# List schedule of a gated mix kernel: rank of the gate scores, planned transfer rate and slack behind a landing

## The chip, the core and the metric

The kernel runs on one core of a Trainium2 chip. The metric is the device time of one execution in microseconds (us). TensorE is called PE, VectorE DVE, ScalarE ACT, GpSimd POOL and SyncE SP, as in the profile; SP and POOL are here the queues that start transfers.

## The reference

With x = A_u of 2048 tokens and 512 channels, the reference computes a gate per token, a long convolution per channel (S4D), and a bilinear GLU of width 1792, and mixes the two:

```
g = sigmoid((x * gate_w).sum(-1))
K = 2 * Re(sum_n C * dt * exp(A * dt * pos))        # per channel, 128 states, 2048 positions
a = irfft(rfft(K, 4096) * rfft(x.T, 4096))[:2048].T + x * D_skip
b = ((x @ w_gate) * (x @ w_up)) @ w_down
out = g * a + (1 - g) * b
```

## The kernel before

Two streams of work share the engines. The GLU is the larger. Its products run in three passes of a high and a low part of each operand: per tile of hidden units, `pg` and `pu` are sums over four 128-row pieces kt of `xs,wlo` and `xs,whi` (three matmuls of 128x512 for each piece, 0.227 us from start to start), ACT copies pg into h, DVE multiplies h by pu, ACT casts h to hh, and DVE subtracts (`hl<-h,hh`). Then `y` collects `dhi,hl`, `dlo,hh` and `dhi,hh` for each of the hidden tiles of a group. There are two banks for y, one each for pg and pu, and four for all that is named `k`. ACT evicts y as `acc<-y,ngate`, scaled by 1 - g of its token rows, so the first evictions wait for the gate. Tokens come as `raw` or `ts`, are split by ACT (a cast) and DVE (a subtract) into `xs`, go out to `xs_d` in DRAM once and come back from there later. Weights come as `raw` (256 KB, two buffers), are cast by ACT to `whi` or `dhi`, and their low parts are made on POOL's queue or on DVE (`dlo<-kt,dhi` at the start).

The convolution is the other stream. From `pb` (parameters) DVE and ACT make tables of powers (`t`, `rt`, `ri`, `e`, `su`, `di`, `sq`, `x`, `v`; steps with such names and `m` are DVE's products), PE makes from them the kernel values (`k<-v,x`), DVE folds these into `kt` (the last step is `kt<-kt,skip`), and PE transforms them (`k<-kt,w1k_t`), as it does u (`k<-in,w2s`); products, an inverse transform and the mix follow, up to the end.

The function `u_part(t)` handles four row blocks of u, for t from 0 to 3. It loads 1 MB into `in`, takes four gate scores on DVE (`score_of`, line 736: one scalar_tensor_tensor for each with an accumulated sum, `y,gate<-in,w3s`), makes the sums and differences `y<-in` (two, 128x1024) and `in<-y` (four, 128x512), and transforms them on PE. ACT then takes a tanh of the scores and DVE makes `ngate` and `gate` from it (`gates`, line 801). The pool of `y` tiles that the scores write as a by-product is that of the sums, with two buffers.

Nothing of this is issued directly. Every step is a Task with an engine, a planned duration, a rank, an earliest time and the tiles that it reads and writes. `Work.run` (line 301) plans all of them: again and again it takes, over all engines, the task with the smallest tuple of planned start, rank and number, and books its end. The order in which tasks are taken is the order in which each engine issues them, and `InOrder` (line 119) pins that order; so all instructions show line 124. A lower rank wins only among tasks with the same planned start. Transfers are booked on a planned bus with the duration bytes / DMA_RATE, and a task of PE, ACT or DVE that reads a landing is planned SURE later than the planned landing (`ready`, line 252, for transfers that start after 20 us). These numbers act on the order alone; on the chip every instruction starts when its inputs are there and its engine is free.

```
        if d.dma and d.start > 20.0 and task.engine in ("pe", "act", "dve"):
            return d.end + self.SURE
```

Of the kernel before, what the change touches and what calls it, by code (L numbers as in the profile page):

```python
# [169 lines left out]
class Bus:  # L170
# [18 lines left out]
    def add(self, task, at, us):  # L189
        at = max(at, self.now)  # L190
        self.serve(self.queues, self.now, at)
        self.now = at
        self.queues[task.engine == "pool"].append([task, us])
        return self.serve([[[*x] for x in q] for q in self.queues], at, 1e9)


class Work:
# [13 lines left out]


    APART, LESS = 6.0, 4.0
    DMA_RATE = 0.33

    SENT = {"sp": 0.9, "act": 0.9, "pool": 1.4}
    LANDED = {"sp": 1.0, "act": 1.0, "pool": 1.3}
    SURE = 2.0

    def __init__(self):  # L220
        self.tags, self.tasks = {}, []
# [30 lines left out]
    def ready(self, task, d):  # L252
# [3 lines left out]
        if d.dma and d.start > 20.0 and task.engine in ("pe", "act", "dve"):  # L256
            return d.end + self.SURE
        return d.end + self.LAG.get(task.engine, 0.03) + (self.PE_LAG if d.engine == "pe" else 0.0)
# [42 lines left out]
    def run(self):  # L301
# [10 lines left out]
        while any(left.values()):  # L312
# [35 lines left out]
            if t.dma:  # L348
                for d, end in bus.add(t, t.end - 0.42 + self.SENT[t.engine], t.dma / self.DMA_RATE / 1000):
                    d.end = end + self.LANDED[d.engine]  # L350
# [14 lines left out]
def gated_mix_kernel(  # L365
# [39 lines left out]
    def new(pool, tag, shape, dtype=F32, bufs=1, loose=False):  # L405
        return work.tile(pools[pool], tag, shape, dtype, bufs, loose)

    def bank():
        return new("ps_k", "k", [P, D], bufs=4, loose=True)


    def inp(shape):
        return new("mid", "in", shape, bufs=2)
# [8 lines left out]
    m_gate = work.memory()  # L422
# [9 lines left out]
    gw = new("mid", "w3s", [P, D], bufs=2)  # L432
# [298 lines left out]
    def u_part(t):  # L731
        ut = inp([P, 4, D])
        rs = slice(4 * t, 4 * t + 4)
        add("sp", 0.42, lambda: sp.dma_start(ut.t, uv[:, rs, :]), w=[ut], dma=1024, after=6.0 + (U_STEP + 1.0) * t)

        def score_of(j):
            r = 4 * t + j
            pr = new("mid", "y", [P, D], bufs=2)
            add(
                "dve", 0.73,  # L740
                lambda: dve.scalar_tensor_tensor(
                    pr.t, ut.t[:, j, :], 1.0, gw.t, op0=ALU.mult, op1=ALU.mult, accum_out=gate[:, r : r + 1]
                ),
                r=[ut, gw], w=[pr, (m_gate, ("s", t))], rank=0,
            )

        for j in range(4):
            score_of(j)
        ones = [new("mid", "y", [P, 2, D], bufs=2) for _ in range(2)]
        ops = (ALU.add, ALU.subtract)  # L750
        for y, op in zip(ones, ops):
            add(
                "dve", 1.22,
                lambda y=y, op=op: dve.tensor_tensor(out=y.t, in0=ut.t[:, :2], in1=ut.t[:, 2:], op=op), r=[ut], w=[y],
            )
        for s, op in enumerate(ops):
            for d, y in enumerate(ones):
                add(
                    "dve", 0.69,
                    lambda d=d, s=s, y=y, op=op: dve.tensor_tensor(  # L760
                        out=ut.t[:, 2 * s + d], in0=y.t[:, 0], in1=y.t[:, 1], op=op
                    ),
                    r=[y], w=[(ut, 2 * s + d)],
                )

        def first(s):
            banks, st = [bank() for _ in range(4)], new("mid", "ev", [P, KT, 4, P], bufs=2)

            def fn():
                for p in range(2):  # L770
                    col, src = 64 * (p + s), 2 * s + (p + s) % 2
                    for tq in range(4):
                        lanes = slice(32 * tq, 32 * tq + 32)
                        pe.matmul(
                            banks[tq].t[64 * p : 64 * p + 64], w1_t.t[lanes, col : col + 64], ut.t[lanes, src],
                            start=True, stop=True, tile_position=(32 * tq, 64 * p),
                        )

            add("pe", 1.3, fn, r=[(ut, 2 * s), (ut, 2 * s + 1), w1_t], w=banks, rank=1, hold=[st])
            for tq in range(4):  # L780
                add(
                    "act", 0.59,
                    lambda tq=tq: act.copy(st.t[:, :, tq], banks[tq].t.rearrange("p (f d) -> p f d", f=KT)),
                    r=[banks[tq]], w=[(st, tq)],
                )
            n0 = 16 * s + 4 * t
            for q in range(KT):
                add(
                    "pool", 0.95,
                    lambda q=q: pool_q.dma_start(  # L790
                        su_d[q, :, n0 : n0 + 4, :], st.t[:, q],
                    ),
                    r=[st], w=[(m_su, (q, n0))], dma=256,
                )

        for s in range(2):
            first(s)
        sc, ga = (m_gate, ("s", t)), (m_gate, t)
        add("act", 1.5, lambda: act.activation(gate[:, rs], gate[:, rs], AF.Tanh, scale=0.5), r=[sc], w=[sc], rank=0)

        def gates():
            dve.tensor_scalar(ngate[:, rs], gate[:, rs], -0.5, 0.5, op0=ALU.mult, op1=ALU.add)
            dve.tensor_scalar(gate[:, rs], gate[:, rs], 0.5, 0.5, op0=ALU.mult, op1=ALU.add)

        add("dve", 0.4, gates, r=[sc], w=[ga, sc], rank=0)
# [684 lines left out]
```

## Time and profile before

| | us |
|---|---|
| median of three runs (586.51, 587.12, 587.54) | 587.12 |
| profiled execution | 588.43 |
| span of the profiled execution | 586.6 |
| PE busy in it | 576.4 |
| DVE busy | 511.3 |
| ACT busy | 399.0 |

The granted TensorE clock is full speed over the whole span. In the rows further down a line of a timeline gives the start, the duration, the engine, the line of the program, the operation, its output and inputs by the program's names, the shape and how many follow each other; square brackets hold the idle time of the engine ahead of it and what ended that. Durations of neighbours on DVE overlap by some hundredths, so the distance of two starts is what one costs.

### The profile page before, as it was taken

Reading aid. Unit: us, or ns where it says so; the run is one execution under the profiler, and the core shown is the slowest. Engines: PE = TensorE matmul, PEld = TensorE weight load, DVE = VectorE, ACT = ScalarE, POOL = GpSimd, SP = SyncE. Lnnn points to the kernel's source line nnn. Section 1 sums busy time; section 2 is a strip of 40 time slices with the busy share of each in tenths; the row PEclk is TensorE's granted clock in tenths of the full one; section 3 lists DMA queues with packets and bytes.
Section 4 is the critical chain, followed back from the end, with each engine's and each line's share of the span. In section 5 each row is a group of like instructions: output and inputs, shape, how many; then the busy total and the mean of one; then the engine's idle time right before and its main releaser. Section 6 shows DMA issues by size and latency. Waiting matters only on the chain.

```text
span 586.6 us, 14827 instructions
## 1 busy us (share of the span) xinstructions
PE 576.4 (98%) x5996; PEld 433.9 (74%) x5996; DVE 511.3 (87%) x812; ACT 399.0 (68%) x891; POOL 113.4 (19%) x159
## 2 busy tenths in 40 slices
PE   8999999999989999999999999999999999999997
PEld 5777777877876777887777778777878787677775
DVE  6998999999999999999799999995999982367664
ACT  5468888898578589876968764899696523443351
POOL 0002222311102231310412200421321104011011
PEclk9999999999999999999999999999999999999999
DMA  8999969997647698998697859899958349899976
GB/s 276 383 369 357 374 241 319 289 257 212 125 154 181 194 272 205 228 245 297 135 257 249 183 180 304 158 187 276 221 136 212 65 143 230 290 270 253 283 159 125
DMA packets 71687, 136.28 MB, mean 232 GB/s; under 512 B 6852, under 2 KB 35780, under 8 KB 69188
## 3 DMA queue, kind: packets, MB, share of 16 engines
q1 hardware_dynamic: 47668, 87.10, 43.0%
q0 software_dynamic: 23392, 47.98, 39.5%
q8 instruction: 47, 0.77, 0.6%
q10 hardware_dynamic: 560, 0.26, 0.2%
q14 instruction: 20, 0.16, 0.1%
HBM read 80.27 MB, written 55.05 MB: 231 GB/s over the span
## 4 chain that ended last, share of the span: by engine, by line
PE 83%; DVE 6%; ACT 4%; DMA 4%; issue 1%; SPq 0%; DVEq 0%; ACTq 0%
PE pg L124 23%; PE pu L124 23%; PE y L124 22%; PE k L124 16%; DVE v L124 1%; DMA pb<-par_d 1%; DMA xs_d<-xs 1%; DVE x L124 1%; DMA y<-in_xT 1%; DMA xs<-xs_d 1%; ACT acc L124 1%; DVE t L124 1%; ACT ev L124 1%; ACT xs L124 1%; ACT e L124 1%
## 5 line engine op out<-in xcount | busy, mean ns | idle before, releaser
L124 PE MATMUL pg<-xs,whi 128*128 128x512 f32 x448 | 138.9, 391 | 1.0 <-DVE xs L124 0.6
L124 PE MATMUL pu<-xs,whi 128*128 128x512 f32 x448 | 138.3, 390 | 0.0
L124 PEld LDWEIGHTS pg<-xs,whi 128*128 128x128 f32 x448 | 84.2, 188 | 20.2 <-ACT whi L124 2.0
L124 PEld LDWEIGHTS pu<-xs,whi 128*128 128x128 f32 x448 | 84.2, 188 | 16.9
L124 PE MATMUL y<-dhi,hl 128*128 128x512 f32 x224 | 90.3, 403 | 2.9 <-DVE hl L124 2.4
L124 PE MATMUL pu<-xs,wlo 128*128 128x512 f32 x224 | 90.1, 402 | 0.0
L124 PE MATMUL pg<-xs,wlo 128*128 128x512 f32 x224 | 89.4, 399 | 0.4 <-ACT h L124 0.4
L124 PE MATMUL y<-dlo,hh 128*128 128x512 f32 x224 | 87.5, 391 | 0.0
L124 PE MATMUL y<-dhi,hh 128*128 128x512 f32 x224 | 87.3, 390 | 0.0
L124 POOL DMA_DIRECT2D out<-acc x44 | 40.2, 968 | 180.4 <-ACT acc L124 173.0
L124 ACT COPY ev<-k 128x512 f32<-128x512 f32 x112 | 58.8, 596 | 14.5 <-PE k L124 14.4
L124 ACT CAST hh<-h 128x512 fp32r<-128x512 f32 x56 | 34.6, 618 | 45.7 <-DVE h L124 45.5
L124 PEld LDWEIGHTS y<-dhi,hl 128*128 128x128 f32 x224 | 42.0, 187 | 24.4 <-issue 8.1
L124 DVE TENSOR_TENSOR h<-pu,h 128x512 f32<-128x512 f32 x56 | 38.5, 688 | 23.6 <-PE pu L124 23.0
L124 PEld LDWEIGHTS pu<-xs,wlo 128*128 128x128 f32 x224 | 42.0, 187 | 20.0 <-issue 10.7
L124 ACT ACTIVATE acc<-y,ngate 128x512 f32<-128x512 f32 x62 | 41.7, 685 | 21.9 <-PE y L124 18.9
L124 PEld LDWEIGHTS pg<-xs,wlo 128*128 128x128 f32 x224 | 42.1, 188 | 18.4 <-issue 6.9
L124 ACT COPY h<-pg 128x512 f32<-128x512 f32 x56 | 32.9, 587 | 28.3 <-PE pg L124 22.0
L124 PEld LDWEIGHTS y<-dhi,hh 128*128 128x128 f32 x224 | 42.1, 188 | 9.1
L124 PEld LDWEIGHTS y<-dlo,hh 128*128 128x128 f32 x224 | 42.1, 188 | 8.2 <-DVE dlo L124 0.3
L124 DVE TENSOR_TENSOR hl<-h,hh 128x512 fp32r<-128x512 f32 x56 | 38.4, 686 | 3.0 <-ACT hh L124 2.7
L124 PEld LDWEIGHTS k<-v,x 128*32 128x32 f32 x2048 | 30.6, 109 | 6.4 <-issue 4.7
(130 smaller groups left out, 965.4 us busy)
## 6 DMA issues: line engine op xcount, KB each, us to landing
xs<-xs_d SPq DMA_DIRECT2D x36, 512.0 KB, 5.8
out<-acc POOLq DMA_DIRECT2D x44, 256.0 KB, 5.9
raw<-in_wts SPq DMA_DIRECT2D x33, 256.0 KB, 5.6
xs_d<-xs SPq DMA_DIRECT2D x16, 512.0 KB, 6.6
su_d<-ev POOLq DMA_DIRECT2D x32, 256.0 KB, 6.3
y_d<-ts SPq DMA_DIRECT2D x28, 256.0 KB, 4.9
in<-su_d POOLq DMA_DIRECT2D x12, 512.0 KB, 5.9
sk_d<-ev SPq DMA_DIRECT2D x6, 1024.0 KB, 5.4
```

The lines of the kernel that those rows point to most:

```text
L124: got = getattr(self.engine, name)(*args, **kw)
```

## The change

Three numbers are changed. The planner books transfers at 0.34 instead of 0.33 (256 KB in 0.75 instead of 0.78 planned us). A reader of a landing is planned 1.0 us behind it instead of 2.0. The gate scores of u have rank 1 instead of 0, the rank of most steps of the convolution; the steps of the GLU on DVE (h, hl, xs, and gates) keep rank 0.

```
@@ class Work
-    DMA_RATE = 0.33
+    DMA_RATE = 0.34
...
-    SURE = 2.0
+    SURE = 1.0
@@ u_part, score_of
-                r=[ut, gw], w=[pr, (m_gate, ("s", t))], rank=0,
+                r=[ut, gw], w=[pr, (m_gate, ("s", t))], rank=1,
```

The set of instructions is the same. The order differs on every engine over most of the program.

DVE, from the second gate score of the first u part to its gates (25 to 34 us). `y,gate<-in,w3s` is a score, `dlo<-kt,dhi` the low part of a weight, `x<-x` a step of the power tables. Before:

```order
L124 SCALAR_TENSOR_TENSOR y,gate<-in,w3s 128x512
L124 TENSOR_TENSOR dlo<-kt,dhi 128x512
L124 SCALAR_TENSOR_TENSOR y,gate<-in,w3s 128x512
L124 TENSOR_TENSOR dlo<-kt,dhi 128x512
L124 TENSOR_TENSOR h<-pu,h 128x512
L124 TENSOR_TENSOR xs<-ts,xs 128x512
L124 TENSOR_SCALAR ngate<-gate 128x4
L124 TENSOR_SCALAR gate<-gate 128x4
```

In the change:

```order
L124 SCALAR_TENSOR_TENSOR y,gate<-in,w3s 128x512
L124 TENSOR_TENSOR xs<-ts,xs 128x512
L124 SCALAR_TENSOR_TENSOR x<-x 128x512
L124 SCALAR_TENSOR_TENSOR y,gate<-in,w3s 128x512
L124 TENSOR_TENSOR xs<-ts,xs 128x512
L124 SCALAR_TENSOR_TENSOR x<-x 128x512
L124 TENSOR_TENSOR xs<-ts,xs 128x512
L124 SCALAR_TENSOR_TENSOR y,gate<-in,w3s 128x512
L124 TENSOR_TENSOR y<-in 128x1024 x2
L124 TENSOR_SCALAR ngate<-gate 128x4
L124 TENSOR_SCALAR gate<-gate 128x4
```

The scores now stand between xs and x<-x, and ngate follows both y<-in; ahead of the rows shown an x<-x, three dlo, h, an xs, x<-x, hl and x<-x come between the first score and the second. On PE 15 matmuls of pg and pu more stand ahead of the third pair of y groups there.

At 50 to 54 us DVE had h alone between `t<-rt,t` and `ri<-t,e`, and now has two xs, h, an xs, an xs from raw, and hl there; on ACT two casts of xs and one of hh, which stood behind the `t<-t` that this ri reads, stand ahead of it.

DVE around 142 us, up to the hl that the y group at 142.35 of the profile reads. Before:

```order
L124 TENSOR_TENSOR t<-pb,turns 128x672
L124 TENSOR_TENSOR h<-pu,h 128x512
L124 TENSOR_TENSOR v<-v,sq 128x32x16
L124 TENSOR_TENSOR su<-ri 128x576
L124 TENSOR_TENSOR hl<-h,hh 128x512
L124 SCALAR_TENSOR_TENSOR v<-v 128x32x8
L124 TENSOR_TENSOR v<-v,sq 128x32x8
L124 TENSOR_TENSOR di<-ri 128x352
L124 TENSOR_TENSOR sq<-pb,ri 128x192 x2
```

In the change:

```order
L124 TENSOR_TENSOR v<-v,sq 128x32x16
L124 TENSOR_TENSOR su<-ri 128x576
L124 SCALAR_TENSOR_TENSOR v<-v 128x32x8
L124 TENSOR_TENSOR v<-v,sq 128x32x8
L124 TENSOR_TENSOR h<-pu,h 128x512
L124 TENSOR_TENSOR di<-ri 128x352
L124 TENSOR_TENSOR sq<-pb,ri 128x192 x2
L124 TENSOR_TENSOR hl<-h,hh 128x512
L124 TENSOR_TENSOR x<-sq 128x32x3 x2
L124 TENSOR_TENSOR t<-pb,turns 128x672
```

Five operations (v, v, di and two sq) moved ahead of hl, and t<-pb,turns behind it.

PE at 171 to 178 us; the first y shown is the one at 173.91 of the profile. Before:

```order
L124 MATMUL pg<-xs,wlo 128x512
L124 MATMUL pg<-xs,whi 128x512 x2
L124 MATMUL y<-dhi,hl 128x512
L124 MATMUL y<-dlo,hh 128x512
L124 MATMUL y<-dhi,hh 128x512
L124 MATMUL y<-dhi,hl 128x512
L124 MATMUL y<-dlo,hh 128x512
L124 MATMUL y<-dhi,hh 128x512
L124 MATMUL pg<-xs,wlo 128x512
L124 MATMUL pg<-xs,whi 128x512 x2
L124 MATMUL k<-kt,w1k_t 128x512 x8
```

In the change:

```order
L124 MATMUL pg<-xs,wlo 128x512
L124 MATMUL pg<-xs,whi 128x512 x2
L124 MATMUL k<-kt,w1k_t 128x512 x8
L124 MATMUL y<-dhi,hl 128x512
L124 MATMUL y<-dlo,hh 128x512
L124 MATMUL y<-dhi,hh 128x512
L124 MATMUL y<-dhi,hl 128x512
L124 MATMUL y<-dlo,hh 128x512
L124 MATMUL y<-dhi,hh 128x512
L124 MATMUL pg<-xs,wlo 128x512
L124 MATMUL pg<-xs,whi 128x512 x2
```

The batch `k<-kt,w1k_t` (eight rows of the order, sixteen records in the trace) moved ahead of the two y groups. On DVE the hl of the first of these groups now has `kt<-kt,skip` and `m<-su,ri` ahead of it, which stood behind.

## Rows read from the trace of the kernel before

**Rows 1.** The page's part 1: busy us, share of the span, instructions.

```profile
PE 576.4 (98%) x5996; PEld 433.9 (74%) x5996; DVE 511.3 (87%) x812; ACT 399.0 (68%) x891; POOL 113.4 (19%) x159
```

**Rows 2.** The chain that ended last, first 30 us: start, us, piece.

```profile
14.97 2.72 PE pu L124 x12
```

**Rows 3.** PE's waits: us in total, times, longest.

```profile
PE y L124 <- DVE hl L124: 2.4, 2, 1.6
...
PE k L124 <- issue: 0.6, 1, 0.6
```

**Rows 4.** Stretches: us, busy of PE, PEld, DVE, ACT, POOL; clock, DMA share, GB/s.

```profile
120.00:176.00 56.00, 53.63 (x590) 43.57 (x588) 55.52 (x87) 42.75 (x108) 6.17 (x8) 1.00 0.67 182
176.00:290.00 114.00, 114.00 (x1363) 86.10 (x1362) 111.60 (x164) 92.47 (x209) 26.29 (x30) 1.00 0.87 224
```

**Rows 5.** PE's timeline, 26 to 31 us.

```profile
26.86 0.73 PE L124 MATMUL pg<-xs,whi 128*128 128x512 f32 x2 [0.57 <-DVE xs L124]
...
27.66 0.63 PE L124 MATMUL pu<-xs,whi 128*128 128x512 f32 x2
28.34 0.50 PE L124 MATMUL y<-dhi,hl 128*128 128x512 f32 x1
...
30.53 0.39 PE L124 MATMUL y<-dhi,hl 128*128 128x512 f32 x1
```

**Rows 6.** DVE's timeline, 26 to 31 us.

```profile
26.73 0.16 DVE L124 TENSOR_SCALAR ngate<-gate 128x4 f32<-128x4 f32 x1
...
30.61 1.22 DVE L124 TENSOR_TENSOR y<-in 128x1024 f32<-128x1024 f32 x1
```

**Rows 7.** ACT's timeline, the first eviction of y.

```profile
29.34 0.69 ACT L124 ACTIVATE acc<-y,ngate 128x512 f32<-128x512 f32 x1 [0.24 <-PE y L124]
```

**Rows 8.** DVE's timeline, 51 to 54 us.

```profile
51.69 0.69 DVE L124 TENSOR_TENSOR h<-pu,h 128x512 f32<-128x512 f32 x1 [1.18 <-PE pu L124]
53.43 0.86 DVE L124 TENSOR_TENSOR ri<-t,e 128x672 f32<-128x672 f32 x1 [1.04 <-ACT t L124]
```

**Rows 9.** PE's timeline at 142 us and from 171 to 178 us.

```profile
142.35 0.50 PE L124 MATMUL y<-dhi,hl 128*128 128x512 f32 x1 [0.74 <-DVE hl L124]
...
171.66 0.61 PE L124 MATMUL pg<-xs,whi 128*128 128x512 f32 x2
173.91 0.50 PE L124 MATMUL y<-dhi,hl 128*128 128x512 f32 x1 [1.63 <-DVE hl L124]
...
176.17 2.00 PE L124 MATMUL k<-kt,w1k_t 32*128 32x512 f32 x16
```

**Rows 10.** DVE's timeline at 139 to 144 us and at 173 us.

```profile
138.98 0.85 DVE L124 TENSOR_TENSOR t<-pb,turns 128x672 f32<-128x672 f32 x1
...
141.62 0.68 DVE L124 TENSOR_TENSOR hl<-h,hh 128x512 fp32r<-128x512 f32 x1
142.22 0.62 DVE L124 SCALAR_TENSOR_TENSOR v<-v 128x256 f32<-128x256 f32 x1
...
144.16 0.86 DVE L124 SCALAR_TENSOR_TENSOR t<-rt,t 128x672 f32<-128x672 f32 x1
...
173.16 0.69 DVE L124 TENSOR_TENSOR hl<-h,hh 128x512 fp32r<-128x512 f32 x1
173.77 0.27 DVE L124 TENSOR_TENSOR kt<-kt,skip 128x64 f32<-128x64 f32 x1
173.94 1.08 DVE L124 TENSOR_TENSOR m<-su,ri 128x896 f32<-128x896 f32 x1
```

**Rows 11.** DMA issues, 60 to 176 us, then 200 to 300: KB each, median us.

```profile
raw<-in_wts SPq DMA_DIRECT2D x13, 256.0 KB, 5.6
...
raw<-in_wts SPq DMA_DIRECT2D x10, 256.0 KB, 4.6
```

**Rows 12.** ACT's timeline, a cast that reads a landing.

```profile
108.96 0.62 ACT L124 CAST whi<-raw 128x512 fp32r<-128x512 f32 x1 [1.31 <-PE pg L124]
```

**Rows 13.** DVE's timeline, the hl behind that cast.

```profile
114.09 0.69 DVE L124 TENSOR_TENSOR hl<-h,hh 128x512 fp32r<-128x512 f32 x1 [0.65 <-ACT hh L124]
```

## The prediction

> **What bounds the kernel now.** I read the busy times first. TensorE (PE) is busy 98% of the span, VectorE (DVE) 87%, ScalarE (ACT) 68% [rows 1]. A busy share says little about pipelined matmuls, so I went to the chain that ended last: in a stretch without waits twelve matmuls take 2.72 us, one start every 0.227 us [rows 2]. The change alters neither the number nor the shapes of matmuls, so PE's work is a constant, and only the time that PE stands still can move. The table of waits shows how little that is: the largest item that names an engine is 2.4 us in two waits for hl from DVE, of which the longer is 1.6 [rows 3]. The table by stretches says who comes near to PE: DVE is busy 55.52 of 56 us from 120 on and 111.6 of the next 114 [rows 4]. PE is the bound, and up to about 176 us a DVE without slack decides where PE loses time. So the sum is made of PE's waits, and each is asked of DVE's order.
>
> A rule speaks against this reading. The Trainium skill, page "Perfetto Trace Analysis", section "Identifying the Most-Contended Engine", holds the matmul busy share to be no good measure of the room that is left, and takes the share of the weight loads instead. That is 74% here [rows 1]; by it DVE with 87% would be the bound, the gain would be DVE's own, the 1.0 us of edit 2 below, and the time 586.1, the forecast's upper end. The even starts of [rows 2] side with PE as the bound.
>
> **The change part by part.** The profiled execution took 588.43 us with a span of 586.6; the median of the three runs is 587.12, 1.3 below that execution. The sum is made against the span and the difference is taken off the median. Clock and work stay, so nothing scales.
>
> 1. *Gate scores behind other DVE work, 25 to 36 us.* Rank 1 lets three of the four scores of the first u part fall behind h, hl and xs. In the trace of before PE stands 0.57 for an xs ahead of the matmul at 26.86 (0.73 with the slower restart), and the y at 28.34 starts 0.23 later than two starts of 0.227 behind the pair at 27.66 [rows 5]. The xs and the hl that end these waits now come earlier on DVE: minus 1.0. Against that, ngate moves behind eight operations more of 0.60 each (hl, four x<-x, three xs; 0.60 is the distance of such starts, 173.16 to 173.77 among others) and two y<-in of 1.2: 4.8 + 2.4 = 7.2. So ngate goes from 26.73 to about 33.9 [rows 6, 10]. The first eviction of y, which reads it, began at 29.34 and takes 0.69 [rows 7]; now it begins near 34.2 and frees its bank near 34.9. PE's third y group began at 30.53; it has 15 more matmuls ahead (3.4) and the 1.0 gained, so PE asks for the bank near 32.9. A new wait of about 2.0. What is queued behind the waiting eviction on ACT is the second eviction, an hh and the exponentials; the next hl on DVE needs that hh. Net of this edit at 35 us: plus 1.0 for PE (bounds: 0.0 if the eviction is not the last to be late, 2.0 if the old waits stay).
>
> 2. *DVE's idle time at 50 to 54 us.* Before, DVE stands still 1.18 for the pu of h and 1.04 for ACT's t [rows 8], 2.2 in all. Now six operations of 0.6 (two xs, h, two xs, hl) stand between t<-rt,t and ri<-t,e where only h stood. The two xs ahead of h cover its wait, and DVE, free at 51.69 - 1.18 = 50.5, comes to ri near 50.5 + 3.6 = 54.1. ACT's t, which ended by 53.43, has three casts of 0.6 (two xs, hh) ahead of it now that stood behind: 55.2. That leaves 1.1 idle of 2.2, taken as 1.2 with the hand-over: **1.0 us of DVE time gained**; bounds 1.6 (one cast fewer ahead of t counts) and 0.5 (a cast stands for its landing).
>
> 3. *The wait at 142.35.* PE waits 0.74 there for hl, whose subtract starts at 141.62 [rows 9, 10]. In the new order the five operations that ran from 142.22 to 144.16 (1.94) stand ahead of that hl, and t<-pb,turns (0.85 at 138.98, less the 0.08 by which such operations overlap: 0.77) behind it [rows 10]: 1.17 more, less the 1.0 of edit 2. That y starts 0.2 later: **plus 0.2** (bounds +0.7 and -0.4, from edit 2's). Edit 1 is inside this: PE comes to this y 1.0 later by itself and waits that much less, since the wait of 0.74 with its slower restart held it some 0.9. So edit 1 moves nothing behind 142, unless it costs more than the 1.0.
>
> 4. *The wait at 173.91.* PE waits 1.63 (1.8 against the two starts behind the pair at 171.66, which would bring this y at 172.1): between the last pu and the y that needs its hl PE has only six matmuls of y and three of pg. In the new order the batch k<-kt,w1k_t, 2.00 us long, stands ahead of this y instead of behind the next [rows 9]. Two us cover 1.8. DVE has kt<-kt,skip (0.17 from start to start) and m<-su,ri (1.0) more ahead of this hl [rows 10]: the subtract ends at 173.85 + 1.17 - 1.0 = 174.0, and PE asks for it at 172.1 + 0.2 + 2.0 = 174.3. The batch itself now needs kt<-kt,skip early; hl no longer stands ahead of that, so it ends near 174.04 - 0.6 - 1.0 = 172.4, where PE is at 172.3: 0.1 left. Together **minus 1.7** (bounds -1.8 and -1.2, if DVE's m or a kt comes 0.5 later).
>
> 5. *Transfers at 0.34 and the slack of 1.0.* Nothing is faster on the chip; the planner places readers of a landing up to 1.0 us earlier in their queues. The nearest rows: 13 raw loads of 256 KB between 60 and 176 us took 5.6 in the median, ten between 200 and 300 us 4.6 [rows 11]. One late landing is to be seen in before: ACT's whi<-raw at 108.96 stood 1.31 (the page names pg; the load had landed last), and the hl behind it on DVE stood 0.65 for its hh [rows 12, 13]. So a late landing costs DVE at most 0.65, and PE only where hl has no margin. In the forecast I take 0, because the same number of such casts stands ahead of an hh in both orders as far as I can follow them; bounds 0 and 0.65 for each.
>
> A rule speaks against this edit. The Trainium skill, page "DMA: Bandwidth & Descriptors", section "Latency and other measured facts", has an HBM access at 0.2 us on average and at 2 us under high load. That spread of 1.8 exceeds the remaining slack of 1.0 by 0.8; by it, an estimate, each landing in a busy stretch could come 0.8 late, and with six such the sum would be +3.3 in place of -1.5. The difference of 5.6 and 4.6 in the trace, 1.0, bears a part of it out; what it would do here is the second rival.
>
> Behind 176 us PE runs without a wait worth naming in before (114.00 busy of 114) [rows 4], and its margins to DVE and ACT grow as DVE thins out; I cost the moved work there at nothing. Its cover is DVE's free time; if it is gone, the price is that of an hl wait, 0.65 to 1.8.
>
> Sum: +0.2 - 1.7 = **-1.5 us**. Its span would be 585.1, and 587.12 - 1.5 = **585.6**. With the bounds: +0.7 - 1.7 = -1.0 or +0.2 - 1.2 = -1.0 on one side, -0.4 - 1.8 = -2.2 on the other, so 584.9 to 586.1.
>
> **The rivals.**
> - *No measurable change, about 587.1.* DVE is full from 120 to 176 us, so a wait removed for one hl is given to the next: the y behind 173.91, or the k batch, waits instead. For it: 99% busy DVE, and the same operations in both orders. Against: the batch ahead of y covers the wait with PE's own work, not DVE's. The gain of 1.7 falls to 0.2 and +0.2 stands against it: 587.1 (586.0 to 588.2). It is also what shows if the new order does not reach PE.
> - *Slower, about 589.5.* Landings come later than planned in the stretch without slack, and each holds ACT's cast, the hh behind it, and DVE's hl for 0.65 [rows 12, 13]. The spread of landings, 1.0 between the two rows [rows 11], is as large as the slack that is left. It decides from 1.5 / 0.65, more than two such waits in 60 to 176 us; six of thirteen raw loads give 3.9 - 1.5 = +2.4.
> - *A larger gain, about 583.8.* The gate wait at 35 does not come and edit 2 gives 1.6, so the wait at 142 goes as well (-1.0 in place of +0.2), and PE's stall of 0.63 within a k batch, which has no releaser [rows 3], does not recur: -1.8 -1.0 -0.6 = -3.4.
>
> **How the numbers follow.** Forecast (584.9 to 586.1) 0.48, no change 0.27, slower 0.13, larger gain 0.12. About 0.2%, 1.2 us, is what a measurement can tell from no change: faster is below 585.95, slower above 588.3. Of the forecast some four fifths lie below 585.95 (0.39), the rest within; with the larger gain and 0.05 of the no-change case that is 0.56 faster. Within: 0.09 + 0.21 = 0.30; slower 0.13 and 0.01 from the upper end of no change: 0.14. The range leaves out most of slower and the half of the larger gain that lies lowest: 583.8 to 588.4.
>
> **What would show it.** Edit 1: an eviction on ACT that waits for ngate, and a wait of PE for acc of about 2 us near 33 to 35 us. Edit 2: DVE's idle at 50 to 56 us at 0.6 to 1.7 instead of 2.2. Edit 3: the y near 142 starts between 141.9 and 143.1. Edit 4: no wait for hl over 0.5 near 174. Edit 5: waits of ACT's raw casts behind landings, no more and no longer than 1.3. The forecast is wrong if PE waits over 1 us for hl anywhere between 60 and 290 us, if the first k batches stall on kt, or if PE's lost time behind 290 us grows.

## The result, and the profile after

The change made the kernel slower: 591.25 us against 588.17 for the kernel before in the same set of runs, a ratio of 1.0048 (95% interval 1.0027 to 1.0069). A second set of the same order gave 1.0058 (1.0027 to 1.0089). The forecast was 585.6, with a range up to 588.4. The profiled execution took 592.65, its span 590.8 against 586.6.

The busy times tell nothing: every engine does the same work.

```profile
PE 579.4 (98%) x5996; PEld 436.2 (74%) x5996; DVE 511.8 (87%) x812; ACT 399.1 (68%) x891; POOL 113.3 (19%) x159
```

PE's waits (total, times, longest), against [rows 3]: the two waits for hl of 2.4 us in all are now three of 3.4, with one of 2.8, and ACT's evictions appear.

```profile
PE y L124 <- DVE hl L124: 3.4, 3, 2.8
PE y L124 <- ACT acc L124: 1.9, 2, 1.4
```

PE's timeline at the places of the forecast, against [rows 5, 9]: the old waits at 26.86 and 28.34 have become one of 0.38; the late gates cost 1.41 at 36.27; the wait for hl near 142 has grown from 0.74 to 2.76; the one at 173.91 is gone; a wait for an eviction at 182.25 is new.

```profile
27.74 0.50 PE L124 MATMUL y<-dhi,hl 128*128 128x512 f32 x1 [0.38 <-DVE hl L124]
...
36.27 0.50 PE L124 MATMUL y<-dhi,hl 128*128 128x512 f32 x1 [1.41 <-ACT acc L124]
...
146.06 0.51 PE L124 MATMUL y<-dhi,hl 128*128 128x512 f32 x1 [2.76 <-DVE hl L124]
...
182.25 0.50 PE L124 MATMUL y<-dhi,hl 128*128 128x512 f32 x1 [0.48 <-ACT acc L124]
```

The busy times in three stretches around the wait at 146 (columns as in [rows 4]; the clock is the third number from the end). The granted clock stays at 1.00 while PE stands and falls when PE goes on: 0.57 over the next 4 us, close to the lower of its two levels (1.2 of 2.4 GHz). Most of the ten matmuls there stand 0.43 us apart instead of 0.227.

```profile
143.30:146.00 2.70, 0.00 (x0) 0.00 (x0) 2.70 (x8) 0.62 (x1) 0.00 (x0) 1.00 1.04 249
146.00:150.00 4.00, 3.94 (x10) 3.12 (x11) 3.97 (x8) 2.01 (x3) 1.08 (x2) 0.57 1.02 328
150.00:160.00 10.00, 10.00 (x163) 8.22 (x163) 8.64 (x11) 5.57 (x12) 2.32 (x3) 1.00 0.78 160
```

DVE was busy the whole time that PE stood, so the reason lies earlier. DVE's timeline, against [rows 10], has two idle times that before did not have, both for ACT, 1.63 us in all; and ACT's timeline has the one that made them: the fourth eviction of a token block stood 2.04 us for the landing of an output write, because the three buffers of `acc` were still being written out.

```profile
131.05 0.43 DVE L124 TENSOR_TENSOR kt<-k,kt 128x256 f32<-128x256 f32 x1 [1.23 <-ACT kt L124]
...
133.57 0.69 DVE L124 TENSOR_TENSOR hl<-h,hh 128x512 fp32r<-128x512 f32 x1 [0.40 <-ACT hh L124]
```

```profile
125.93 0.70 ACT L124 ACTIVATE acc<-y,ngate 128x512 f32<-128x512 f32 x1 [2.04 <-DMA out<-acc]
```

The account of the 4.2 us of span, worked out from the starts of PE's matmuls (each distance less 0.227):

| | before | change |
|---|---|---|
| first 15 us | 0.9 | 2.4 |
| waits from 15 to 130 us | 2.2 | 2.7 |
| the wait for hl at 142 or 146 | 0.9 | 3.1 |
| half clock behind it | 0 | 1.4 |
| the waits from 170 to 185 us | 1.8 | 0.6 |
| all the rest, change less before | | -0.2 |

The first line is not the change's: PE's order is the same up to 25 us, and a second profile of the kernel before (below) has 2.7 there. A start that is read off the change's profile is therefore 1.5 us later than the order alone makes it.

### The profile page after: what moved, and what is told of

Same layout as the page of the kernel before. It is cut to its first block, busy times and chain, and to the rows that moved or that the text cites. A ratio compares the mean times of both kernels' runs of the same rounds, so it can differ in the third digit from the quotient of the medians.

```text
span 590.8 us, 14837 instructions
## 1 busy us (share of the span) xinstructions
PE 579.4 (98%) x5996; PEld 436.2 (74%) x5996; DVE 511.8 (87%) x812; ACT 399.1 (68%) x891; POOL 113.3 (19%) x159
## 4 chain that ended last, share of the span: by engine, by line
PE 83%; DVE 8%; ACT 4%; DMA 3%; issue 1%; DVEq 0%; ACTq 0%
PE y L124 23%; PE pg L124 23%; PE pu L124 22%; PE k L124 16%; DVE v L124 2%; DVE x L124 1%; DMA out<-acc 1%; DMA raw<-in_wts 1%; DVE hl L124 1%; DMA y<-in_xT 1%; DVE h L124 1%; DVE y L124 1%; ACT acc L124 1%; DVE m L124 1%; DVE ri L124 1%
```

## Experiments

**One landing wait taken away.** The order of the change is kept in every queue; only the eviction that stood at 125.93 goes four places back on ACT.

```diff
 L124 CAST dhi<-raw 128x512
-L124 ACTIVATE acc<-y,ngate 128x512
 L124 ACTIVATE dlo<-dhi 128x512
 L124 CAST dhi<-raw 128x512
 L124 COPY h<-pg 128x512
 L124 ACTIVATE dlo<-dhi 128x512
+L124 ACTIVATE acc<-y,ngate 128x512
```

> The changed kernel's order with one task moved: the fourth eviction of the last token block in the first group (the acc that stood 2.04 us at 125.93 for the landing of an output write) goes four places further back in ACT's queue; every other queue is as in the change. Theory A (the halved slack put this eviction ahead of its landing, and ACT's standstill came through kt and hh to the hl that PE waited 2.76 us for at 146): ACT does not stand there, DVE's waits for kt (1.23) and hh (0.40) go, PE's wait at 146 falls to about 1.1, the half clock behind it goes, and the time falls by 2.5 to 3.5 us, to a ratio of 0.998 to 1.001. Theory B (the 1.17 us of table work that the new order puts ahead of that hl on DVE makes the wait, whatever ACT does): the wait stays over 2 us and the ratio near 1.005.

The place behaved as theory A said: DVE's idle times at 131 and 133 are gone, the clock stays at 1.00 there, and the y starts after a wait of 1.0:

```profile
143.40 0.50 PE L124 MATMUL y<-dhi,hl 128*128 128x512 f32 x1 [1.03 <-DVE hl L124]
```

The time did not follow: 589.84, ratio 1.0045 (1.0025 to 1.0066). The profile shows why. At 424 us ACT stood for another landing, the dlo on DVE stood for ACT, h stood behind the dlo, and PE stood 2.37 us for h; behind that the clock was 0.66 for 5 us. First ACT's line, then DVE's, then PE's wait and a stretch behind it:

```profile
424.24 0.62 ACT L124 CAST dhi<-raw 128x512 fp32r<-128x512 f32 x1 [3.09 <-DMA raw<-in_wts]
```

```profile
424.89 0.69 DVE L124 TENSOR_TENSOR dlo<-raw,dhi 128x512 fp32r<-128x512 f32 x1 [2.70 <-ACT dhi L124]
```

```profile
426.24 0.50 PE L124 MATMUL pu<-xs,wlo 128*128 128x512 f32 x1 [2.37 <-DVE h L124]
```

```profile
426.00:431.00 5.00, 4.76 (x43) 2.91 (x43) 4.65 (x6) 1.21 (x2) 0.00 (x0) 0.66 0.00 0
```

In the change's own profile that cast had no wait at all. So the loss has no fixed place, and taking one place away is not shown to gain anything.

**Single parts.** Each is the kernel before with some of the three numbers changed.

```diff
-    DMA_RATE = 0.33
+    DMA_RATE = 0.34
...
-    SURE = 2.0
+    SURE = 1.0
...
-                r=[ut, gw], w=[pr, (m_gate, ("s", t))], rank=0,
+                r=[ut, gw], w=[pr, (m_gate, ("s", t))], rank=1,
```

Rank and rate without the slack:

> The change without its slack edit: rank 1 and rate 0.34, slack 2.0. Theory A (the slack is to blame): no wait of ACT for a landing over 1 us between 60 and 176 us, no wait of PE for hl over 2 us, ratio 0.997 to 1.001. Theory C (the rank, through the late gates, is to blame): a wait of PE for acc near 36 us of 1.5 and a ratio of 1.003 or more.

The slack alone:

> Before with the slack of 1.0 alone. Theory A: ACT waits for landings over 1 us between 60 and 176 us, PE waits for hl more than in before, ratio 1.002 to 1.008. Theory C: like before, ratio 0.998 to 1.002.

The rate alone:

> Before with the rate of 0.34 alone. Theory A: the 3% shorter planned transfers take some 0.1 us off each planned landing, so no landing wait worth naming: ratio 0.997 to 1.002. Theory C expects the same. A ratio over 1.003 would say that any reshuffled order loses, and that neither the slack nor the rank is the cause by itself.

The rank alone:

> Before with the rank of the scores at 1 alone. The planner's own end for this order is 588.3 against 576.7 for before and 576.2 for the change (576.9 for the slack alone, 575.5 for the rate alone). If the planned end carries weight: slower than before by 6 to 12 us, ratio 1.010 to 1.020. If it carries none: 591 to 595 like the other single edits.

The planner's own end is the us at which its plan has the last task done.

| numbers changed | planner's own end | ratio to before | interval |
|---|---|---|---|
| none | 576.7 | 1 | |
| all three | 576.2 | 1.0048 | 1.0027 to 1.0069 |
| rate | 575.5 | 1.0080 | 1.0063 to 1.0098 |
| rank and rate | 576.0 | 1.0111 | 1.0078 to 1.0143 |
| slack | 576.9 | 1.0115 | 1.0097 to 1.0133 |
| rank | 588.3 | 1.0212 | 1.0186 to 1.0238 |

Every part is slower than the whole. Theory A as I had it (the halved slack is to blame) falls: without the slack edit the loss is larger, not gone. Theory C (the rank) falls too as the only cause, since the slack and the rate lose without it.

Rank and rate also counts against landings as the only cause. Theory A asked for no landing wait over 1 us from 60 to 176 us and no wait for hl over 2 us there; both came true and the time was still 593.33. In its profile (593.05) no task of ACT behind 60 us stood for a landing longer than 0.95, and the clock stayed at 1.00. PE's waits there are spread: 1.38 for acc at 36.74, 1.25 and 1.07 for hl at 145.16 and 176.14, 0.72 for h at 268.56, and two stops without a named releaser, 0.84 at 554.82 and this one:

```profile
440.57 0.61 PE L124 MATMUL k<-v,x 128*32 128x64 f32 x20 [1.07 <-issue]
```

Which of them makes the 1.1% is not shown. The slack alone does show the same eviction standing for the same write:

```profile
127.43 0.69 ACT L124 ACTIVATE acc<-y,ngate 128x512 f32<-128x512 f32 x1 [1.91 <-DMA out<-acc]
```

and the rate alone, whose planned end is the lowest of all, has two casts that stand for raw loads, one 1.71 at 120.57 and one 2.41, where before stood 0.70 at most between 60 and 290 us for any landing that the profile names. Behind the second DVE's hl stood 2.22 for its hh, and PE 0.60 for an h:

```profile
264.08 0.62 ACT L124 CAST dhi<-raw 128x512 fp32r<-128x512 f32 x1 [2.41 <-DMA raw<-in_wts]
```

The planner's end tells a difference of 2% (the rank alone, where 13 us follow the last matmul instead of 4) and nothing of the smaller ones, up to 1.15%.

**Both orders with light transfers.** This separates landings from the engines' own work: the accumulating transfers of GpSimd's queue are cut to an eighth in both kernels, and both orders stay as they are. In the light change the loads of raw between 60 and 176 us take 3.7 us in the median instead of 5.0.

```diff
-add("pool", 0.95, lambda: pool_q.dma_start(lo.t, src, accum_op=ALU.add), ...
+add("pool", 0.95, lambda: pool_q.dma_start(lo.t[:, :64 * n], src[:, :64 * n], accum_op=ALU.add), ...
-lambda: pool_q.dma_start(ov[:, t, :], acc.t, accum_op=ALU.add),
+lambda: pool_q.dma_start(ov[:, t, :64], acc.t[:, :64], accum_op=ALU.add),
```

> The kernel before, each accumulating transfer of GpSimd's queue cut to an eighth of its columns (44 sums into the output, the low parts wlo and dlo of the later weights), so that most of those sums are left out; order and all other work are kept. Landings come earlier. PE stays the bound: 585.5 to 588, no wait of ACT for a raw load.

> The changed kernel with the same transfers cut to an eighth (the same sums left out). Landing theory: the waits of ACT for raw and for the output write at 115 to 130, 243 to 268 and 424 to 430 go, PE's wait at 146 falls to about 1.2, and the time is within 0.3% of the light kernel before (585 to 588.5). Order theory (the engines' own work makes the loss): still 2.5 to 3.5 us above the light kernel before.

Before went to 586.56 (ratio to the full kernel before 0.9972, 0.9958 to 0.9985), the change to 587.33 (0.9987, 0.9973 to 1.0002): the loss of 0.48 to 0.58% is down to 0.15%, and the two intervals overlap. A second set of the light change, beside other executions of the kernel before, gave 0.9997 (0.9983 to 1.0011), which leaves 0.25%. In the profile of the first set no line of ACT from 60 to 290 us stands for a transfer, the wait near 143 is 1.00 and the clock stays:

```profile
142.86 0.50 PE L124 MATMUL y<-dhi,hl 128*128 128x512 f32 x1 [1.00 <-DVE hl L124]
```

So between half and 70% of the loss hangs on the transfers that were cut, and ACT's landing waits go with them. What is left, 0.8 to 1.5 us, is not told apart from none by the first pair.

The profiles show where it sits: not in the stretch of the forecast. With equal work of PE done (worked out from the starts of its matmuls) and the first 20 us set aside, the light change is level with light before at 290 us, or 0.2 ahead in the second set. It falls behind between 310 and 340 us (0.6 and 1.2) and between 478 and 500 (0.8 and 1.5), in batches of small k matmuls where no engine and no transfer is named. Two executions of one order differ there as well, the two of the light change by 0.6 and 0.7, the two of the kernel before by 0.3 and 1.0, so it is open whether this belongs to the order.

**Two more tasks moved in the full order.** To the late eviction comes the dhi cast of 424 us behind the next hh (and its dlo behind the next hl), and then early gates.

```diff
-L124 CAST dhi<-raw 128x512
 L124 CAST hh<-h 128x512
+L124 CAST dhi<-raw 128x512
```

> The first experiment's order with a second move of the same kind: the fourth dhi cast near 424 us, which stood 3.09 us for its raw load there, goes behind the next hh on ACT, and its dlo behind the next hl on DVE. Theory A (tasks that the plan places too close behind a landing, each in a queue with an hh or h behind it, make the loss): PE has no wait over 1.5 us between 60 and 575 us, the clock stays at 1.00, the median falls to 587 to 589, ratio 0.998 to 1.003. If the loss is spread over many small waits: ratio 1.004 or more, with the waits elsewhere.

> The order of the experiment before with the gates early: three gate scores move ahead of three x<-x on DVE, ngate ahead of the second y<-in, and the first two evictions of y ahead of the next h on ACT. The forecast's step (what the late gates cost at 36 us is taken back at 142, where DVE sets the time): the wait of PE for acc of 1.6 to 2.3 at 36 goes, the wait for hl near 143 grows by as much, and the time stays within 0.4 us of the experiment before. Rival: the 1.6 to 2.3 reach the end, ratio 0.003 to 0.004 lower than the experiment before.

The first gave 589.65, 1.0024 (1.0008 to 1.0041), half of the loss with two tasks moved; its seven executions and an interval that overlaps the change's (1.0027 to 1.0069) do not show the half. PE's wait at 426 is gone; its profile has its half clock at 36 instead (0.60 from 36 to 40 us, behind a wait for acc of 2.0). The second took the wait at 36 down to 0.60 and still gave 590.77, 1.0044 (1.0028 to 1.0060); its profile has 2.7 us in the first 15 us and casts that stand 1.16 and 1.90 for raw loads at 116 and 267. With six executions it does not price the gates either way.

**The change and before again.**

> The changed kernel's order, word for word, for a second profiled execution. If what cost time in the first one sits in the order: the wait of PE for acc near 36 of 1.5 or more and the wait of ACT's fourth eviction for its landing near 126 (over 1 us) come again, with the wait for hl near 146 over 2 us and half clock behind it. If it sits in that one execution: some of them are gone, and the first 15 us take some 1.4 us less, as in most other profiles. Ratio 1.003 to 1.007 either way.

> The kernel before, unchanged, as a control for what two sets of runs of one program differ by: ratio 0.998 to 1.002. In its profile the waits for hl at 142 (0.9) and at 174 (1.8) come again and no stretch behind 15 us is at half clock; the first 15 us cost 0.7 to 2.9 us over the even pace, whichever the execution brings.

Before again is 1.0006 (0.9988 to 1.0024); its waits at 142 and 174 come again to a few hundredths, its landing waits are 0.47 and 0.29. The change again was half as expected: the wait for acc came again (2.15 at 36.08), this time with the half clock behind it, and so did the eviction near 126 (1.11); the wait for hl at 146.12 was 1.84, and the clock stayed behind it. It stood for landings in places where it had not: among ACT's lines in its second profile are these five, and the last two made PE stand 1.66 at 269.5 and 1.2 at 430. The longest, for whi, made no wait of PE: an eviction and table steps stood behind it on ACT, no h and no hh.

```profile
125.99 0.69 ACT L124 ACTIVATE acc<-y,ngate 128x512 f32<-128x512 f32 x1 [1.11 <-DMA out<-acc]
156.98 0.69 ACT L124 ACTIVATE acc<-y,ngate 128x512 f32<-128x512 f32 x1 [2.09 <-DMA out<-acc]
...
243.81 0.62 ACT L124 CAST whi<-raw 128x512 fp32r<-128x512 f32 x1 [3.14 <-DMA raw<-in_wts]
...
268.37 0.62 ACT L124 CAST dhi<-raw 128x512 fp32r<-128x512 f32 x1 [2.82 <-DMA raw<-in_wts]
...
428.36 0.62 ACT L124 CAST dhi<-raw 128x512 fp32r<-128x512 f32 x1 [1.88 <-DMA raw<-in_wts]
```

**Early gates on the light change.** On DVE the scores go ahead of x<-x, on ACT the first two evictions ahead of the next h.

```diff
-L124 COPY h<-pg 128x512
 L124 ACTIVATE acc<-y,ngate 128x512 x2
+L124 COPY h<-pg 128x512
```

> The light changed kernel with the early gates (three scores ahead of three x<-x, the first two evictions ahead of the next h; the same sums left out). Forecast's step (absorbed at 142): the wait for acc at 36 falls from 1.6 to 2.3 to under 0.8, the wait for hl near 143 grows by about as much, time within 0.5 us of the light changed kernel, lower by up to 1.6 more in the executions where the clock fell behind 36. Rival: lower by 1.6 to 2.3 throughout.

> The light changed kernel with the gates ahead of two x<-x and both y<-in on DVE, and the first two evictions ahead of the next h on ACT (the same sums left out). The wait for acc near 36 should fall from 1.9 to under 0.5. Forecast's step (absorbed at 142): the wait for hl near 143 grows from 1.0 to 2 or more and the y there starts within 0.4 us of 142.9; time within 0.6 us of the light changed kernel beside it. Rival: that y starts 1.4 us or more earlier and the time falls by as much.

> The light changed kernel again (the same sums left out), for the comparison on one chip and for a second profiled execution: 586.5 to 588, the wait for acc near 36 of 1.6 to 2.3, the wait for hl near 143 of about 1.0, no wait of ACT for a raw load or an output write behind 60 us.

The first failed: three x<-x still stood ahead of the gates, PE stood 1.95 as before, and half clock behind it in that execution made it slower (589.0). The second removed the wait at 36. Its y near 143 starts at 142.99 against 142.70 in the light change beside it, and the times are 587.75 and 588.13, within their scatter. The wait came back at once, before 142: the moved y<-in made the first transform of u late. So it does not test whether a wait at 36 is taken back at 142.

```profile
39.89 1.69 PE L124 MATMUL k<-in,w2s 32*64 32x512 f32 x16 [1.65 <-DVE in L124]
...
142.99 0.50 PE L124 MATMUL y<-dhi,hl 128*128 128x512 f32 x1 [1.00 <-DVE hl L124]
```

**Matmuls that fill the wait at 146.** Ten copies of the first product of the next pg ahead of the y.

```diff
+L124 MATMUL pg<-xs,wlo 128x512 x10
 L124 MATMUL y<-dhi,hl 128x512
```

> The changed kernel's order with ten extra matmuls on PE (the first product of the next pg, ten times over, 2.27 us) ahead of the y that waited 2.76 us for hl at 146. Nothing else is moved. Clock theory (PE's standstill made the granted clock fall to 0.54 to 0.61 for the 4 us behind it, at a cost of about 1.8 us): PE stands under 1 us there, no stretch near 146 shows a clock under 1.00, the matmuls behind keep 0.227 us, and the time falls by 1 to 2 us from the change's 591.25. If the clock falls for another reason, the stretch at half clock stays and the time is that of the change or up to 1 us more.

592.02, ratio 1.0069 (1.0050 to 1.0087). In the profiled execution the eviction near 126 stood only 0.37, so the ten matmuls had no wait to fill, and the y behind them started at 147.67 without one. The half clock stood behind the late gates instead (0.57 from 36 to 40 us). It decides nothing on the clock.

**Reading hl last.** In each y the products with hh come first.

```diff
-            for n, (a, b) in enumerate(THREE):
+            for n, (a, b) in enumerate(((0, 1), (0, 0), (1, 0))):
```

> The kernel before with the three products of each y in the order hh, hh, hl in place of hl, hh, hh; the order of everything else is the same. PE then asks for hl 0.45 us later. If PE's waits for hl are what can still be won: the waits at 142 and 174 fall by 0.45 each, 118 by 0.3, time lower by about 1 us, ratio 0.997 to 0.999. If DVE takes it back: 1.000.

> The kernel before with hl read last in each y, a second time: ratio 0.996 to 0.9995 as in the first set if the gain is real, 1.000 if it was scatter.

> The third order experiment (late eviction, late dhi, early gates) with hl read last as well. If the change has a gain of its own behind its three bad places: the waits at 118 (1.4), 146 (1.2) and 28 (0.5) fall by 0.45 each, 588 to 589.5, ratio 0.999 to 1.003. If it has none, it stays at 1.003 to 1.005.

On the kernel before 587.26, 0.9978 (0.9960 to 0.9995), then 588.56, 0.9997 (0.9984 to 1.0011): the gain did not come again, so no version is shown to beat the kernel before. The waits did shrink (0.25 instead of 0.72 at 143, 0.57 and 0.31 instead of 1.62 at 174). On the moved order it gave 1.0063 (1.0043 to 1.0083); a cast stood 3.10 for a raw load at 243 there, but PE had no wait behind it, so that loss is not explained.

## Why the prediction was wrong

- **Edit 5, the step that failed.** The forecast took 0 for landings, with an upper end of 0.65 each, from one row [rows 12, 13], and gave that rival 0.13. Two parts of the price were missing. The unit is not 0.65: the eviction at 125.93 stood 2.04, the dhi in the first experiment 3.09, as ACT stood each time until the transfer had landed. And it is passed on almost in full where the next operation of DVE waits too and PE's h or hl stands behind (2.70 and 2.37 at 424). Counting six small waits was the wrong picture: in the change's two profiles and in the first experiment one or two large ones, in different places, made PE stand 1.2 to 2.8 us each. I had also counted raw casts alone; the output write that holds an `acc` buffer is a landing that ACT waits for as well. With the transfers cut, half of the loss or more was gone.
- **"Clock and work stay, so nothing scales"** failed beside it. Behind a standstill of PE half clock cost 1.4 to 1.8 us more. In the two sets of the change, 12 of 26 executions have a mean clock of 0.994 to 0.997 and a median of 592.8 us; the other 14 have 589.6, only some 1.3 above before. That the fall of the clock makes this difference fits the traces; no run tested it, since the one meant to had no wait to fill.
- **That slack is the cause** was the rival's reading and is not borne out: rank and rate with the full slack lose 1.1%, and without a landing wait over 0.95. The halved slack is one way to a tight place; what costs in each other order is shown for none of them by a test.
- **Edit 1** was right in the size of the wait: forecast 2.0 for the gates at 36, measured 1.4 to 2.1. The 1.0 to be gained at 26 to 28 was 0.4 in the change's profile and little or nothing in the others. What was missing is the half clock behind this wait, in three of the five profiles with this order of the gates and full transfers (0.57 to 0.60 from 36 to 40 us): there PE fell behind the kernel before by 3.3 to 3.7 us between 25 and 45 us, at equal work done, in the other two by 0.7 and 1.6. So not every half clock in the change hangs on a landing. That nothing of edit 1 reaches beyond 142 holds for the first experiment and the light change, which had no half clock there.
- **Edit 2** was mis-sized: the idle time left at 50 to 58 us is 0.18 + 0.31 + 1.20 = 1.7, forecast 1.2, so 0.5 was gained, the lower end. The last of the three:

```profile
58.01 0.86 DVE L124 TENSOR_TENSOR ri<-t,e 128x672 f32<-128x672 f32 x1 [1.20 <-ACT t L124]
```

- **Edit 3**: forecast 0.2 later than before for that y, at most 0.7. With the first 20 us set aside it was 2.2 later with the landing wait, 0.9 without it in the first experiment, and 1.0 to 1.2 later than in light before with light transfers. The 1.17 of work moved ahead of hl is all there; the 1.0 against it was not.
- **Edit 4** held: no wait for hl or for the batch at 174 in any profile of the change's order, a gain of 1.8. The wait for an eviction at 182.25, 0.48 (0.6 from start to start) and in all of these profiles, was not looked for.
- Without landings and half clock the sum is +0.9 to +1.2 at 142, with the late gates inside it, and -1.8 + 0.6 behind it: near nothing in place of -1.5. The first experiment and the light change agree: at 190 us, with the first 20 us set aside, they are 0.0 to 0.3 ahead of the order before.

What stays open: the 0.8 to 1.5 us between the light kernels, and why the order of the kernel before meets its landings so much better than five neighbours of it. Its loads were not faster (5.6 us in the median between 60 and 176 us, 5.0 in the change), and its order is not free of such waits: with hl read last, where ACT's order is the same, a dhi cast stood 2.06 for its load at 118.26 in one execution, and PE 1.42 for the eviction behind it.

## What to carry to other kernels

Where a queue in program order holds a task that reads a landing, ask for the latest landing and not the median one (loads into raw between 60 and 300 us took 5.3 to 5.4 us in the median, the longest 9.0 in the change and 11.7 in before), and count what stands behind it: an h or an hl there handed most of the wait to the engine that bounds the kernel (2.37 of 3.09), while 3.14 us with neither behind it cost it nothing. Where a new order is tight to landings one profile does not show; two profiles of the same order stood in different places here. To find the cause in a planned order, move single tasks and keep the rest: changing one of the planner's numbers gave a new order each time, and every part alone was slower than the whole.

## What the runs showed of the hardware

- The granted clock fell to about half behind these standstills of PE (start to start, over the even pace): 2.93 at 146.06 in the change (0.57 over 4 us), 2.53 at 426.24 in the first experiment (0.66 over 5 us), 2.27 at 145.64 in the slack alone (0.57 over 4 us), 2.11 to 2.33 at 36 in four executions (0.57 to 0.63 over 4 us). It stayed at 1.00 behind 2.26 at 36 in the first experiment, 2.05 at 429.30 in the order with ten extra matmuls, 2.00 at 146.12 in the change again and 1.79 at 174 in before. The half clock cost 1.4 to 1.8 us each time, so a wait of 2 us can become one of nearly 4. Of some 130 executions of the kernel before with a clock on record, one has a mean under 0.999.
- In the first 10 us PE's matmuls came 0.43 us apart until 6.7 us in some executions and until 9.7 or 10.6 us in others, of both kernels alike (0.7 to 0.9 or 2.2 to 2.9 us over the even pace). The row of the clock gives 1.00 there, and so does the mean over the whole span, but the trace holds no record of the clock for this stretch: its first record, at full speed, begins at 6.78 us in before and at 9.89 in the change, where the even pace begins.
- Transfers cut to an eighth on one queue brought the loads of another from 5.0 to 3.7 us in the median in the change's order, and from 5.6 to 3.6 in that of before.
